# Decode attention mixed with a feed-forward branch: three small weight loads cut into sixteen pieces each

## The chip, the cores and the metric

The kernel runs on one core of one Trainium2 chip. The metric is the device time of one execution in microseconds (us); of several executions the median is shown.

## What is computed

One token, two branches, and a gate between them (the reference, cut to what matters):

```python
x = A_x                                              # 1 x 1 x 512
g = sigmoid((x * gate_w).sum(-1))
q = (x @ wq).reshape(1, 1, 32, 128)                  # 32 heads of 128
s = einsum("bhqd,bhkd->bhqk", q, k_cache) * 128 ** -0.5   # 65536 keys a head
p = softmax(s)
o = einsum("bhqk,bhkd->bhqd", p, v_cache)
a = o.reshape(1, 1, 4096) @ wo                       # wo: 4096 x 512
b = (silu(x @ w_gate) * (x @ w_up)) @ w_down
out = g * a + (1 - g) * b
```

All data are bf16. The caches are 32 heads x 65536 positions x 128 numbers each for keys and for values: 512 MiB each, a gigabyte together, and every byte of them is used once. Everything else is small beside that; `wo` has 4 MB.

## The kernel before, in words

**Tiles.** A head's keys are cut into four tiles, so there are 128 key tiles and 128 value tiles. Each is 128 partitions x 16384 numbers, 4 MB, and is fetched by one transfer (`load`, line 103, the issue is line 109). Every partition's share is one stretch of 32 KB in memory. All big tiles come from one pool of five buffers (`ring`, line 58), so a load has to wait until an earlier tile has been used up.

**Work on a key tile** (step n): VectorE multiplies it by the query (`products`, line 218) and folds 128 columns to 16 by three additions (line 222). TensorE adds up the rest with an identity matrix into the scores (`scores`, line 232). When a head's four tiles are through, its softmax follows (lines 243 to 272) on VectorE, ScalarE and TensorE.

**Work on a value tile** (step v): TensorE multiplies it by the probabilities, 32 matmuls (`values`, line 280). After a head's four value tiles, `head_out` (line 289) gathers the head's output into `oT`, and `project` (line 309, matmul line 310) multiplies it by the rows of `wo` that belong to the head and adds that to the sum `a_ps`.

**The order is written out by hand** (lines 319 to 370). A step issues the load of key tile n, then (in some steps) a load of `wo`, then the load of value tile v, and then the work. All loads are issued by SyncE, in this order, on one queue. SyncE does nothing else: an issue that has to wait holds up everything that is issued after it.

**The load of wo.** `wo` is fetched in eight groups of four heads (`load_wo`, line 143; the issue is line 146). A group is a tile of 128 partitions x 4 x 512 numbers, 512 KB: partition p gets, for each of four heads, one row of 1 KB. There are two such buffers (line 61). Group 0 is loaded at the start (line 148). The others are loaded in the loop (lines 334 and 335), when v is 8 more than a multiple of 16, thus eight value tiles before the first head that needs the group. In the queue this transfer stands between a key tile and a value tile.

**Semaphores.** Nothing in the kernel's text says which semaphore a transfer uses; the layer that builds the program deals them out. In the built program the transfers that SyncE issues take turns on eight semaphores, called DMAHW0 to DMAHW7. Where a semaphore's previous transfer isn't known to have landed, the next transfer on it is issued only when it has.

Of the kernel before, what the change touches and what calls it, by code (L numbers as in the profile page):

```python
# [11 lines left out]
P = 128  # L12
# [7 lines left out]

LAG = 8
SPREAD = 40


@with_exitstack
def kernel(
# [14 lines left out]
    nc = tc.nc  # L41
# [3 lines left out]
    _, H, Sk, Dh = A_k_cache.shape  # L45
# [94 lines left out]
    WG = 4  # L140
    wo_tiles = {}

    def load_wo(g):
        wo_tiles[g] = wo_pool.tile([P, WG, D], bf16, name="wo_sb")
        rows = A_wo[g * WG * P : (g + 1) * WG * P, :]
        nc.sync.dma_start(out=wo_tiles[g], in_=rows.rearrange("(h p) n -> p h n", p=P))

    load_wo(0)

    def feed_forward_in():  # L150
# [170 lines left out]
    for n in range(N):  # L321
        due = n >= G and not (n >= SPREAD and n % 4 == 3 and n - v < LAG)
        steps.append((n, v if due else None))
# [6 lines left out]
    for n, v in steps:  # L330
        if n is not None and n > 1:
            load(K_tiles, A_k_cache, n, "K_t")
        if v is not None:
            if v % (WG * G) == 2 * G and v // (WG * G) + 1 < H // WG:
                load_wo(v // (WG * G) + 1)
            load(V_tiles, A_v_cache, v, "V_t", (0, NB) if v < N - 1 else (0, 64, 96, 112, NB))
# [70 lines left out]
```

## Time and profile before

| what | value |
|---|---|
| median of 3 runs | 2549.31 us (2547.87 to 2550.05) |
| profiled execution, its own time | 2551.07 us |
| its span, first to last instruction | 2549.3 us |
| moved by the DMA engines | 1088.61 MB, mean 427 GB/s |
| VectorE busy | 2175.0 us, 85% |
| TensorE matmul busy | 1736.2 us, 68% |
| ScalarE busy | 75.7 us, 3% |
| key and value loads | 4096 KB each, median 35.4 and 29.6 us from issue to landing |
| loads of wo | 8 of 512 KB, median 36.3 us from issue to landing |
| share of the chain that ended last | DMA 66%, TensorE 22%, VectorE 11% |

The span is what lies between the first and the last instruction; the execution's own time is 1.8 us longer. "Landing" is the moment at which the last part of a transfer has been reported by its semaphore. The time from issue to landing is mostly time in the queue behind earlier transfers. Engines are named as in the profile: PE is TensorE, DVE is VectorE, ACT is ScalarE, SP or SPq is SyncE and its queue. An L with a number is a line of the kernel.

### The profile page before, as it was taken

What the parts mean: (1) busy time and instruction counts of PE and PEld (TensorE: products, weight loads), DVE (VectorE), ACT (ScalarE), POOL (GpSimd) and SP (SyncE); (2) the same over time, 40 slices, a digit from 0 to 9 for tenths busy, and PEclk for the clock granted to TensorE, in tenths of its full rate; (3) what the DMA queues carried; (4) which work ended last, traced back from release to release, by engine and by line L of the source; (5) the groups of instructions that cost most, each with busy time, mean ns of one, the idle gap of its engine ahead of it and who ended that gap; (6) DMA issues with size and microseconds to landing.
All of it is one profiled execution on the core that took longest, in us unless ns stands there. A gap on an engine that the chain in (4) does not pass through costs nothing.

```text
span 2549.3 us, 15203 instructions
## 1 busy us (share of the span) xinstructions
PE 1736.2 (68%) x6722; PEld 707.5 (28%) x6722; DVE 2175.0 (85%) x780; ACT 75.7 (3%) x206; POOL 0.7 (0%) x6
## 2 busy tenths in 40 slices
PE   3576666776776666666676776677667676776678
PEld 2232222222232222222222222222222222232223
DVE  6999888888888999998888888888888888888860
ACT  1000000000000000000000000000000000000000
POOL 0000000000000000000000000000000000000000
PEclk7677767777777677777776777767777777777779
DMA  9999999999999999999999999999999999999997
GB/s 407 427 432 430 430 433 429 433 428 431 432 431 431 428 431 431 432 430 432 430 430 433 429 432 429 433 429 432 431 429 433 429 433 428 433 430 432 430 434 304
DMA packets 42451, 1088.61 MB, mean 427 GB/s; under 512 B 4625, under 2 KB 8722, under 8 KB 8978
## 3 DMA queue, kind: packets, MB, share of 16 engines
q1 hardware_dynamic: 42386, 1087.66, 99.4%
q8 instruction: 52, 0.85, 0.1%
q14 instruction: 13, 0.11, 0.0%
HBM read 1087.64 MB, written 0.00 MB: 427 GB/s over the span
## 4 chain that ended last, share of the span: by engine, by line
DMA 66%; PE 22%; DVE 11%; issue 1%; ACT 0%; SPq 0%; DVEq 0%; ACTq 0%
DMA V_t<-in_A_v_cache_dram 60%; PE O_ps L280 20%; DVE K_t L218 6%; DMA K_t<-in_A_k_cache_dram 5%; DVE K_t L222 5%; PE S_ps L232 1%; DMA wq_t<-in_A_wq_dram 0%; PE qg_ps L118 0%; PE oh_ps L298 0%; DVE m L244 0%; ACT P_sb L257 0%; PE a_ps L205 0%; ACT O_sb L293 0%; DVE top L253 0%; PE a_ps L310 0%
## 5 line engine op out<-in xcount | busy, mean ns | idle before, releaser
L280 PE MATMUL O_ps<-V_t,P_sb 128*4 128x512 bf16 x4096 | 1156.4, 452 | 501.6 <-DMA V_t<-in_A_v_cache_dram 499.3
L218 DVE TENSOR_TENSOR K_t<-K_t,q_bc 128x16384 bf16<-128x16384 bf16 (+1 forms) x159 | 1117.2, 7026 | 275.3 <-DMA K_t<-in_A_k_cache_dram 272.1
L222 DVE TENSOR_TENSOR K_t<-K_t 128x2048 bf16<-128x2048 bf16 (+3 forms) x477 | 1030.6, 2161 | 14.2
L280 PEld LDWEIGHTS <-P_sb 128*4 128x4 bf16 x4096 | 394.0, 97 | 1244.4 <-issue 900.2
L232 PE MATMUL S_ps<-K_t,ident_b 128*128 128x128 bf16 x2048 | 464.5, 392 | 119.0 <-DVE K_t L222 119.0
L232 PEld LDWEIGHTS <-ident_b 128*128 128x128 bf16 x2048 | 225.7, 114 | 342.1 <-issue 149.2
L298 PE MATMUL oh_ps<-ident_f,O_sb 4*128 4x1 f32 x256 | 57.1, 340 | 73.1 <-ACT O_sb L293 73.1
L248 PE MATMUL mT_ps<-diag,ones_f 128*128 128x128 f32 x64 | 25.0, 494 | 78.3 <-ACT diag L246 78.3
L298 PEld LDWEIGHTS oh_ps<-ident_f,O_sb 4*128 4x128 f32 x256 | 54.4, 310 | 83.2 <-ACT O_sb L293 78.9
L246 ACT ACTIVATE diag<-ident_f,m 128x128 f32<-128x128 f32 x32 | 12.9, 402 | 2108.8 <-DVE m L244 2108.8
L295 DVE COPY O_sb<-O_ps 4x256 f32<-4x256 f32 x1 | 0.4, 413 | 56.5 <-ACT O_sb L293 56.5
L248 PEld LDWEIGHTS mT_ps<-diag,ones_f 128*128 128x128 f32 x64 | 15.7, 305 | 94.0 <-ACT diag L246 94.0
L244 DVE TENSOR_REDUCE m<-S_ps 128x1 f32<-128x512 f32 x32 | 21.9, 684 | 7.6 <-PE S_ps L232 7.6
L293 ACT ACTIVATE O_sb<-O_ps 4x512 f32<-4x512 f32 (+1 forms) x32 | 18.1, 565 | 135.4 <-PE O_ps L280 135.4
L257 ACT ACTIVATE P_sb<-S_ps,bias 128x512 bf16<-128x512 f32 x32 | 22.0, 687 | 1.0
L118 PE MATMUL qg_ps<-wq_t,X_bc 128*128 128x512 bf16 x32 | 8.8, 443 | 14.0 <-DMA wq_t<-in_A_wq_dram 14.0
L183 PE MATMUL b_ps<-wd_t,hT 128*1 128x512 bf16 x14 | 6.1, 626 | 15.7 <-DVE hT L176 15.7
L271 DVE RECIPROCAL recip<-tot_ps 128x1 f32<-128x1 f32 x32 | 5.1, 160 | 12.4 <-PE tot_ps L266 12.4
L310 PE MATMUL a_ps<-wo_sb,oT 128*1 128x512 bf16 x32 | 13.3, 416 | 0.4 <-ACT oT L305 0.4
L266 PEld LDWEIGHTS tot_ps<-rowsum,ones_f 128*128 128x128 f32 x64 | 9.5, 188 | 14.0 <-issue 14.0
L266 PE MATMUL tot_ps<-rowsum,ones_f 128*128 128x1 f32 x64 | 12.2, 260 | 0.0
L305 ACT ACTIVATE oT<-oh_ps,rg 128x1 bf16<-128x1 f32 x32 | 8.4, 264 | 75.3 <-PE oh_ps L298 75.3
(38 smaller groups left out, 62.4 us busy)
## 6 DMA issues: line engine op xcount, KB each, us to landing
K_t<-in_A_k_cache_dram SPq DMA_DIRECT2D x128, 4096.0 KB, 35.4
V_t<-in_A_v_cache_dram SPq DMA_DIRECT2D x127, 4096.0 KB, 29.6
wq_t<-in_A_wq_dram SPq DMA_DIRECT2D x1, 4096.0 KB, 12.3
wo_sb<-in_A_wo_dram SPq DMA_DIRECT2D x8, 512.0 KB, 36.3
V_t<-in_A_v_cache_dram SPq DMA_DIRECT2D x1, 2048.0 KB, 31.4
gu_t<-in_B_w_gate_dram SPq DMA_DIRECT2D x1, 1792.0 KB, 34.6
gu_t<-in_B_w_up_dram SPq DMA_DIRECT2D x1, 1792.0 KB, 38.4
wd_t<-in_B_w_down_dram SPq DMA_DIRECT2D x1, 1792.0 KB, 42.2
```

What stands on the lines that cost most here:

```text
L218: yield nc.vector.tensor_tensor(out=K, in0=K, in1=q_rep, op=ALU.mult)
L222: yield nc.vector.tensor_tensor(out=K[:, :, 0:half], in0=K[:, :, 0:half], in1=K[:, :, half : 2 * half], op=ALU.add,)
L232: nc.tensor.matmul(S_tiles[h][:, g * NB : (g + 1) * NB], lhsT=ident_b, rhs=K_tiles[n][:, :, c], start=(c == 0), stop=(c == WIDTH - 1),)
L244: nc.vector.tensor_reduce(out=m, in_=S_tiles[h], axis=AXIS.X, op=ALU.max)
L246: nc.scalar.activation(out=diag, in_=ident_f, func=ACT.Copy, scale=m)
L248: nc.tensor.matmul(mT_ps, lhsT=ones_f, rhs=diag, start=True, stop=True)
L257: nc.scalar.activation(out=P_tiles[h], in_=S_tiles[h], func=ACT.Exp, bias=bias, scale=scale, accum_out=rowsum[:, h : h + 1],)
L266: nc.tensor.matmul(tot_ps, lhsT=ones_f, rhs=rowsum[:, h : h + 1], start=True, stop=True)
L280: nc.tensor.matmul(O_tiles[h], lhsT=P_tiles[h][:, g * NB + j : g * NB + j + 4], rhs=V_tiles[n][:, j : j + 4, :], start=(g == 0 and j == 0) ...
L293: nc.scalar.activation(out=O_sb[:, :cut], in_=O_ps[:, :cut], func=ACT.Copy)
L298: nc.tensor.matmul(oh_ps, lhsT=O_sb[:, c * Dh : (c + 1) * Dh], rhs=ident_f[0:4, c : c + 1], start=(c == 0), stop=(c == 3),)
L310: nc.tensor.matmul(a_ps, lhsT=oT[:, h : h + 1], rhs=wo_tiles[h // WG][:, h % WG, :], start=False, stop=(h == H - 1),)
```

## The change

Groups 5, 6 and 7 of `wo` are no longer fetched by one transfer of 128 partitions each, but by sixteen transfers of eight partitions each (32 KB). Groups 0 to 4 are as they were. Destination, data and place in the order are the same.

```diff
+NARROW = 3
...
     def load_wo(g):
         wo_tiles[g] = wo_pool.tile([P, WG, D], bf16, name="wo_sb")
         rows = A_wo[g * WG * P : (g + 1) * WG * P, :]
-        nc.sync.dma_start(out=wo_tiles[g], in_=rows.rearrange("(h p) n -> p h n", p=P))
+        rows = rows.rearrange("(h p) n -> p h n", p=P)
+        step = P if g < H // WG - NARROW else 8
+        for a in range(0, P, step):
+            nc.sync.dma_start(out=wo_tiles[g][a : a + step], in_=rows[a : a + step])
```

`H // WG` is 8. In the changed kernel the issue of a load of `wo` is line 151, and that of a key or value load is line 111.

## The prediction

> **What bounds the kernel now.** I read the page's slices and queues first, to see which resource never rests; then SyncE's timeline around a load of wo, with the landing of each transfer, since the change lies there; then the chain of waits over the same stretch; last the built order of both kernels, which says what each issue waits for.
>
> The page, sections 2 and 3:
>
> ```profile
> DMA  9999999999999999999999999999999999999997
> q1 hardware_dynamic: 42386, 1087.66, 99.4%
> ```
>
> The 16 DMA engines are busy in every slice, and SyncE's queue alone fills 99.4% of them. VectorE, the next, has 85%. A microsecond in which the DMA engines have nothing to do is a microsecond on the end, unless the queue can later run faster than it does now.
>
> SyncE's timeline around group 5 of wo (start, duration, what):
>
> ```profile
> 1489.65 0.33 SPq L109 DMA_DIRECT2D V_t<-in_A_v_cache_dram  x1
> 1493.21 0.33 SPq L109 DMA_DIRECT2D K_t<-in_A_k_cache_dram  x1
> 1493.59 0.43 SPq L146 DMA_DIRECT2D wo_sb<-in_A_wo_dram  x1
> 1507.92 0.33 SPq L109 DMA_DIRECT2D V_t<-in_A_v_cache_dram  x1
> 1511.48 0.33 SPq L109 DMA_DIRECT2D K_t<-in_A_k_cache_dram  x1
> 1527.87 0.33 SPq L109 DMA_DIRECT2D V_t<-in_A_v_cache_dram  x1
> ```
>
> The landings of the first five, asked for one by one, took 29.1, 35.3, 36.4, 31.8 and 37.9 us from issue. So they landed at 1518.75, 1528.5, 1530.0, 1539.7 and 1549.4 us: a 4 MB tile every 9.7 us, and 1.5 us for wo. The queue is never empty: when the key tile lands at 1528.5, wo, a value tile, a key tile and another value tile (issued 1527.87) are already behind it. Groups 6 and 7 show the same picture at 1807.56 and 2121.51 us.
>
> The chain of waits over this stretch:
>
> ```profile
> 1489.65 29.10 DMA V_t<-in_A_v_cache_dram
> 1518.75 0.04 issue
> 1518.79 9.06 PE O_ps L280 x32
> 1527.85 0.02 issue
> 1527.87 31.25 DMA V_t<-in_A_v_cache_dram
> ```
>
> A value tile lands, TensorE uses it in 9.06 us, and that frees the buffer for the next value load but one. This loop looks like a TensorE step in the chain, but its long part is time in a full queue.
>
> **The change, part by part.** The order of PE, DVE, ACT and POOL is the same in both built programs; only SyncE's differs: three issues go, 48 come.
>
> *The issues alone.* 16 issues at wo's 0.43 us plus about 0.05 between issues (1493.21 to 1493.59 is 0.38 for an issue of 0.33) are 7.7 us. SyncE is free from 1494.0 to 1507.9, 13.9 us, in the old kernel. Without waits this costs nothing; uncovered, SyncE would be late by 7.7 us with over 20 us of work queued, still nothing.
>
> *The waits.* The built order of the changed kernel shows what matters (the semaphore that an issue waits for, in brackets; each of the three groups is alike):
>
> ```
> L111 K_t   [DVE, PE]
> L151 wo 0  -            wo 1 [DMAHW5]   wo 2  -           wo 3 [DMAHW7]
> L151 wo 4  [DMAHW0]     wo 5 [DMAHW1]   wo 6  [DMAHW2]    wo 7 [DMAHW3]
> L151 wo 8  [DMAHW4]     wo 9 [DMAHW5]   wo 10 [DMAHW6]    wo 11 [DMAHW7]
> L151 wo 12 [DMAHW0]     wo 13 [DMAHW1]  wo 14 [DMAHW2]    wo 15 [DMAHW3]
> L111 V_t   [DMAHW4, PE]
> L111 K_t   [DMAHW5, DVE, PE]
> ```
>
> Eight semaphores are dealt out in turn, and each issue waits for the landing of the transfer eight before it. Tile loads in the old kernel never feel that: fewer than eight are in flight. Sixteen pieces go around twice. Piece 7 is the eighth after the key tile issued just before the group, and waits for that tile to land. Queued behind it on SyncE are eight pieces and then the value and key loads that used to go out at 1507.92 and 1511.48.
>
> Call T0 the landing of that key tile (1528.5 for group 5). Pieces 0 to 6 are issued before T0 and stand in the queue behind the tile. At T0 the queue holds nothing but them.
>
> 1. Piece 7 goes out at T0 + 0.05. Pieces 8 to 14 wait for 0 to 6, which land right behind the tile; 0 to 6 are 7/16 of a transfer that took 1.5 us on 16 engines, so they are through within about 1.5 us even on half the engines, while pieces 8 to 14 leave one by one. Piece 15 waits for piece 7, which by the row of xT (1 KB, 1.8 us from issue to landing) lands near T0 + 2; its turn comes at T0 + 3.9. So nothing waits twice, and nine issues (7 to 15) of 0.48 us take 4.3 us.
> 2. The value load goes out at T0 + 4.4. Its buffer is long free (its old issue, 1507.92, is T0 - 20.6); DMAHW4 is piece 8, landed by T0 + 3.
> 3. Into an idle queue, a 4 MB transfer takes 12.3 us from issue to landing (wq at the start, behind two 1 KB loads). It lands at T0 + 16.7.
> 4. In the old kernel it lands at 1539.7, T0 + 11.2, behind wo's 1.5 us.
> 5. The loss is 5.5 us a group. The pieces' own transfer time lies inside that gap.
>
> After the gap the key load and the next value and key loads follow (their buffers were free at 1511.48, 1527.87 and 1531.42, all before T0 + 5), so four tiles stand in the queue by T0 + 6, and the value load after them waits, as before, for the first one's landing plus 9 us of TensorE. From there all is the old pattern, 5.5 us later. VectorE, with 85%, isn't what could regain it; nor the queue: 32 tiles of 9.7 and a wo of 1.5 are 311.9 us, and groups lie 313.95 us apart. The queue has at most 2 us in 314 to give back, under 6 us for all three groups.
>
> Sum: 3 x 5.5 = 16.5 us. The profiled execution took 2551.07 us, so its like would take 2567.6; it lies 1.76 us above the median, and the forecast on the median's scale is 2549.31 + 16.5 = **2565.8 us**, +0.65%. (About 0.2%, 5.1 us, is what a measurement of this kernel can tell from no change.)
>
> *Bounds of the unknown sizes.* An issue of eight partitions is not in the trace. Below: 0.33 us plus 0.05, as a tile's; above: 0.48 (the early issues) plus 0.05 and 0.02 for a wait (the row of wait instructions on L109 has a median of 17 ns); far above: 1.52, the slowest issue of the run (a key load at 22.84). I take wo's own 0.43, the same three-step pattern. The start into an idle queue: 9.7 plus xT's 1.8 is 11.5 below, wq's 12.3 above. With both low, 3.4 + 0.05 + 11.5 - 11.2 = 3.8 us a group, 11 in all; with both high, 6.1 and 18. The 2 us of slack can take up to 6 off the low end: 2549.3 + 5 to 2549.3 + 18, and more if an issue is dearer.
>
> *How many DMA engines.* The old transfer's 1.5 us are 512 KB on 16 engines. If eight partitions reach only eight, a group takes 3.0 us on these and nothing on the others. In the gap of some 6 us that is hidden; without a gap it would cost between -1.5 us a group (pieces on engines that run ahead) and +1.5. I take 0.
>
> [...]
>
> **The rivals.**
>
> *No wait that counts (not slower).* Piece 7's wait would have to end early: the semaphore would be one whose last transfer had landed by about 1505. The place is that issue; its price is the whole 16.5 us; the deciding point is whether the next value load goes out before T0 - 2 or so, when the queue runs dry. For it: 13.9 us of free SyncE time, and 7.7 us of issues fit. Against it: the built order names DMAHW3, the tile's. It gives 2549.3, between 2545 and 2554 by the engine count.
>
> *Every piece pays a landing.* If pieces 7 to 15 go one after another, 9 x 1.8 = 16.2 us before the value load, 16.2 + 12.3 - 11.2 = 17.3 a group, 52 in all: 2601. For it: each does wait for a landing. Against it: for the one eight before it.
>
> *A dear issue.* At 1.52 + 0.05 us, nine take 14.1: 15.2 a group, 46 in all: 2595. For it: that one row. Against it: 1 KB and one-row issues at 0.39 and 0.32.
>
> **How the numbers follow.** The gap at T0 with a loss of 3 to 8 us a group: 0.83, and 2565.8 us. No wait that counts: 0.07 (0.06 within 0.2%, 0.01 faster). Every piece pays a landing, 0.05; a dear issue, 0.05. The first alone gives the range: 2556 (low sizes and the slack regained) to 2575 (8.5 us a group, an issue of some 0.8 us); 0.80 or a little over lies inside. Slower by over 0.2%: the first but for a corner of 0.02, and the last two: 0.91. Within 0.2%: 0.08. Faster: 0.01.
>
> **What would show it.** SyncE's timeline: seven issues of L151 soon after the key load or as older tiles land, a long pause, then nine in a row from the key tile's landing, 0.4 to 0.5 us apart, and the value load right behind them. The DMA share must dip in three windows, by 5 to 6 us each. The value load should land 12 us after its issue in place of 32. It would be wrong if the nine stand 1.5 us or more apart, if the value load goes out some 14 us after the key load as it does now, or if the queue regains the gap before the end.

## The result, and the profile after

| | before | changed |
|---|---|---|
| median of 6 runs, us | 2548.80 | 2562.80 |
| lowest to highest, us | 2547.87 to 2550.05 | 2561.56 to 2564.55 |
| ratio, 95% interval | | 1.0052 (1.0041 to 1.0062) |
| span of the profiled execution, us | 2549.3 | 2560.7 |

The changed kernel is slower by 14.0 us, 0.52%. The forecast was +16.5 us (2565.8, range 2556 to 2575).

The mean rate of each fortieth of the span, first in the kernel before, then in the changed kernel, and the changed kernel's queue (the page's sections 2 and 3):

```profile
GB/s 407 427 432 430 430 433 429 433 428 431 432 431 431 428 431 431 432 430 432 430 430 433 429 432 429 433 429 432 431 429 433 429 433 428 433 430 432 430 434 304
GB/s 409 427 430 429 432 430 431 432 429 431 431 431 432 428 432 432 430 433 429 431 431 431 431 376 433 429 430 433 389 433 432 431 430 395 431 430 433 432 429 355
q1 hardware_dynamic: 42722, 1087.66, 99.1%
```

The bytes are the same. Apart from the last slice, in which the loads end, three slices drop, to 376, 389 and 395 GB/s: these are the three groups, and between them the rate is what it was. SyncE's queue fills 99.1% in place of 99.4%.

SyncE's timeline around group 5 of the changed kernel (L151 is the load of wo, L111 a tile load; the sixteen pieces are one row, from the first issue to the end of the last):

```profile
1492.83 0.33 SPq L111 DMA_DIRECT2D K_t<-in_A_k_cache_dram  x1
1493.20 38.27 SPq L151 DMA_DIRECT2D wo_sb<-in_A_wo_dram  x16
1531.58 0.36 SPq L111 DMA_DIRECT2D V_t<-in_A_v_cache_dram  x1
1532.04 0.36 SPq L111 DMA_DIRECT2D K_t<-in_A_k_cache_dram  x1
1532.50 0.38 SPq L111 DMA_DIRECT2D V_t<-in_A_v_cache_dram  x1
1532.98 0.47 SPq L111 DMA_DIRECT2D K_t<-in_A_k_cache_dram  x1
```

The value load that went out at 1507.92 goes out at 1531.58, and then four tile loads leave within 1.9 us, because their buffers had been free for a while. What SyncE does in those 38 us is in the chain of waits of the same stretch (start, duration, what):

```profile
1492.83 35.61 DMA K_t<-in_A_k_cache_dram
1528.43 0.02 issue
1528.45 0.27 SPq L151
1528.72 0.04 issue
1528.77 0.30 SPq L151
...
1531.17 0.30 SPq L151
```

The key tile issued at 1492.83 lands at 1528.43 (T0). 0.02 us later SyncE issues piece 7, and then eight more, 0.34 us apart. Only then comes the value load. In the list of SyncE's waits, two rows are new (waiting line, what ended the wait, us in total, times, longest):

```profile
SPq L151 <- DMA K_t<-in_A_k_cache_dram: 57.9, 6, 10.0
SPq L151 <- DMA V_t<-in_A_v_cache_dram: 42.6, 6, 9.4
```

Pieces 4 to 7 of each group wait for tiles to land: twelve waits. The stretch in windows (start and end; busy us and instructions of PE, PEld, DVE, ACT and POOL; granted clock; DMA share; GB/s), first the changed kernel:

```profile
1520.00:1527.00 7.00, 7.00 (x28) 2.52 (x27) 5.32 (x3) 0.00 (x0) 0.00 (x0) 0.82 0.64 240
1527.00:1534.00 7.00, 4.00 (x19) 1.71 (x16) 5.47 (x3) 0.40 (x1) 0.00 (x0) 0.91 0.45 125
```

and the kernel before:

```profile
1520.00:1527.00 7.00, 7.00 (x27) 2.52 (x26) 5.79 (x3) 0.00 (x0) 0.00 (x0) 0.80 0.97 403
1527.00:1534.00 7.00, 4.39 (x20) 1.88 (x18) 5.42 (x3) 0.35 (x1) 0.00 (x0) 0.93 1.01 425
```

The DMA share falls to 0.64 and 0.45 where it was 0.97 and 1.01. It falls before T0 already: the 16 engines don't keep step (the first of the key tile's sixteen marks comes 7.6 us before the last here; see the last section), and those that are ahead run dry first. What counts is the last one, at T0.

The landings are in the trace's records of the semaphores: a tile leaves sixteen marks on its semaphore, and the last of them is its landing (us; T0 is the landing of the key tile before the group):

| group | key tile after the tile before it | value load issued | value tile lands | before: key tile / value tile |
|---|---|---|---|---|
| 5 | +10.17 | T0 + 3.14 | T0 + 15.37 | +9.74 / T0 + 11.19 |
| 6 | +10.14 | T0 + 3.14 | T0 + 15.41 | +9.75 / T0 + 11.17 |
| 7 | +10.24 | T0 + 3.14 | T0 + 15.30 | +9.74 / T0 + 11.18 |

So each group loses 4.2 us after T0 and 0.4 us before it, 13.8 us in three. At the end of the loads the changed kernel is 13.8 us behind, counted from the tile before group 5. The two profiled spans differ by less, 11.4 us: that tile had landed 0.5 us earlier in the changed kernel's trace, and the last 64 value matmuls took 15.66 us in the profiled execution of before, at a granted clock of 0.89, and 13.97 in the other, at 1.00. The medians differ by 14.0.

### The profile page after: what moved, and what is told of

Same layout as the page of the kernel before. It is cut to its first block, busy times and chain, and to the rows that moved or that the text cites. A ratio compares the mean times of both kernels' runs of the same rounds, so it can differ in the third digit from the quotient of the medians.

```text
span 2560.7 us, 15251 instructions
## 1 busy us (share of the span) xinstructions
PE 1734.4 (68%) x6722; PEld 707.1 (28%) x6722; DVE 2175.0 (85%) x780; ACT 75.7 (3%) x206; POOL 0.7 (0%) x6
## 3 DMA queue, kind: packets, MB, share of 16 engines
q1 hardware_dynamic: 42722, 1087.66, 99.1%
## 4 chain that ended last, share of the span: by engine, by line
DMA 67%; PE 21%; DVE 11%; issue 1%; SPq 0%; ACT 0%; DVEq 0%; ACTq 0%
DMA V_t<-in_A_v_cache_dram 58%; PE O_ps L285 19%; DMA K_t<-in_A_k_cache_dram 8%; DVE K_t L223 5%; DVE K_t L227 5%; PE S_ps L237 1%; DMA wq_t<-in_A_wq_dram 0%; PE qg_ps L120 0%; PE oh_ps L303 0%; SPq L151 0%; DVE m L249 0%; ACT P_sb L262 0%; SPq L111 0%; PE a_ps L210 0%; ACT O_sb L298 0%
## 5 line engine op out<-in xcount | busy, mean ns | idle before, releaser
L188 PE MATMUL b_ps<-wd_t,hT 128*1 128x512 bf16 x14 | 6.0, 621 | 15.4 <-DVE hT L181 15.4
L271 PE MATMUL tot_ps<-rowsum,ones_f 128*128 128x1 f32 x64 | 12.2, 260 | 0.0
```

The source lines that it names most:

```text
L271: nc.tensor.matmul(tot_ps, lhsT=ones_f, rhs=rowsum[:, h : h + 1], start=True, stop=True)
```

## The experiments

Theory: the eighth transfer after the key load waits for that tile's landing; the queue drains; then nine issues and the start of a transfer into an idle queue pass before data flow again. Rivals: small pieces or many issues cost in themselves; running on eight of 16 DMA engines is the cost.

All runs change groups 5 to 7 alone unless told otherwise. The last column is how far the last tile's landing lags behind that of before, counted from the tile before group 5; in pool and all7 pieces move before that tile, so none is given.

| run | pieces of a group | median against before, us | ratio, 95% interval | loads' lag, us |
|---|---|---|---|---|
| changed kernel | 16 x 8 partitions | +14.0 | 1.0041 to 1.0062 | 13.8 |
| p6 | 6 of 16 or 32 partitions | +11.8 | 1.0034 to 1.0059 | 10.7 |
| p8 | 8 x 16 partitions | +7.9 | 1.0021 to 1.0043 | 7.7 |
| p32 | 32 x 4 partitions | +29.2 | 1.0100 to 1.0128 | 29.8 |
| cols16 | 16 x 128 partitions | +16.0 | 1.0049 to 1.0074 | 15.8 |
| spread | 16 x 8, two a step | +22.0 | 1.0067 to 1.0095 | 23.6 |
| pool | 16 x 8, by GpSimd | +16.0 | 1.0051 to 1.0076 | |
| all7 | 16 x 8, seven groups | +34.5 | 1.0122 to 1.0150 | |
| spread_stride | 16 x 8, every fourth partition, two a step | +11.2 | 1.0031 to 1.0056 | 11.4 |
| spread_dst | the same, rows read as in spread | +11.2 | 1.0028 to 1.0056 | 11.5 |
| six128 | 6 x 128 partitions | +0.6 | 0.9995 to 1.0012 | 0.3 |
| eight128 | 8 x 128 partitions | +5.1 | 1.0009 to 1.0027 | 4.4 |
| stride16 | 16 x 8, every fourth partition | +23.0 | 1.0077 to 1.0105 | 22.7 |

### First: the number of pieces

```diff
-        step = P if g < H // WG - NARROW else 8
-        for a in range(0, P, step):
-            nc.sync.dma_start(out=wo_tiles[g][a : a + step], in_=rows[a : a + step])
+        cuts = [0, P] if g < H // WG - NARROW else [0, 16, 32, 48, 64, 96, P]   # p6; p8: steps of 16, p32: of 4
+        for a, b in zip(cuts[:-1], cuts[1:]):
+            nc.sync.dma_start(out=wo_tiles[g][a:b], in_=rows[a:b])
```

p6: 

> Groups 5 to 7 of wo in six pieces (four of 16 partitions, two of 32). Theory (the eighth transfer after the last key load waits for that key tile, and the queue runs dry): the value load is the seventh after the key load and waits for nothing late, only the next key load is the eighth; it may go out at the tile's landing with a whole value tile still queued. No dip, median within 3 us of the kernel before (ratio 0.999 to 1.001). Rival (cutting costs in itself, by issues or by small descriptors): 6/16 of the 14 us, about +5 us. [...]

p8: 

> Groups 5 to 7 of wo in eight pieces of 16 partitions. Theory: the eighth piece waits for the key tile (T0), the value load goes out one issue later at T0 + 0.4 us and lands 12.2 us after that, 12.6 against 11.2 before: a gap of 1.4 us a group, +4.2 us in all, in the trace a value load issued 0.4 us after the key tile's landing. Rival (cost by number of pieces): half of 14, +7 us, with the value load issued long before the landing. [...]

p32: 

> Groups 5 to 7 of wo in 32 pieces of four partitions. Theory: after T0 come 25 issues of 0.34 us, 8.5 us, then the value load: 8.5 + 12.2 - 11.2 = 9.5 us a group, +28.6 us in all; the waits of pieces 16 to 31 cost nothing, since eight issues (2.7 us) take longer than a piece's landing (1.9 us). Rival (every piece pays its landing): 25 x 1.9 = 47 us a group, +145. Rival (the drain alone counts, pieces are free): as sixteen, +13.

p32 came out as the theory has it: 25 issues after T0, 0.35 us apart, value load at T0 + 8.7, +29.2 us. Pieces don't pay their landing (1.9 us from issue) one after another. p8 has the value load at T0 + 0.43 as expected, but it costs 7.9 and not 4.2 us: the key tile came 10.7 us after the tile before it, a microsecond late. And p6 contradicts the theory as it stood. Its value load goes out 12.2 us before the key tile lands, the queue never drains, and it is 11.8 us slower all the same. The key tile lands 12.3 to 12.6 us after the tile before it. Something other than a wait is at work there. SyncE's timeline in p6 (T0 is 1530.14):

```profile
1492.29 0.33 SPq L111 DMA_DIRECT2D K_t<-in_A_k_cache_dram  x1
1492.66 15.78 SPq L151 DMA_DIRECT2D wo_sb<-in_A_wo_dram  x6
1517.90 0.35 SPq L111 DMA_DIRECT2D V_t<-in_A_v_cache_dram  x1
1530.21 0.35 SPq L111 DMA_DIRECT2D K_t<-in_A_k_cache_dram  x1
```

```diff
+        cuts = [0, D] if g < H // WG - NARROW else list(range(0, D + 1, D // 4))   # cols16
+        for h in range(WG if len(cuts) > 2 else 1):
+            for a, b in zip(cuts[:-1], cuts[1:]):
+                heads = slice(h, h + 1) if len(cuts) > 2 else slice(0, WG)
+                nc.sync.dma_start(out=wo_tiles[g][:, heads, a:b], in_=rows[:, heads, a:b])
```

cols16: 

> Groups 5 to 7 of wo in sixteen pieces of all 128 partitions (128 columns of one head each, 256 B a row), so every piece reaches all 16 DMA engines. Theory: same order and same waits as sixteen pieces of eight partitions, so the same gap: value load issued some 3 us after the key tile's landing, 4.2 us a group, +12.5 us by landings and 11 to 15 us in the median; a little more if an issue of 128 rows is dearer than 0.34 us. Rival (eight of 16 engines are the cost): most of it gone, under +4 us.

Here every piece is 128 columns of one head and leaves sixteen marks of landing, as a tile does and where the changed kernel's pieces leave eight, so I take it to reach all 16 engines; and the cost is as large, 16.0 us against 14.0. The rival of the eight engines falls as the cause of the gap. The key tile is on time (9.8 us), the value load goes out at T0 + 4.24, since an issue of 128 rows takes 0.47 us and not 0.34.

### Second: the same pieces without the wait

```diff
-        step = P if g < H // WG - NARROW else 8
-        for a in range(0, P, step):
-            nc.sync.dma_start(out=wo_tiles[g][a : a + step], in_=rows[a : a + step])
+        if g < H // WG - NARROW:
+            nc.sync.dma_start(out=wo_tiles[g], in_=rows)
+            return
+        for a in range(0, P, 8):                                    # spread
+            pieces.append((wo_tiles[g][a : a + 8], rows[a : a + 8]))
...
+            for _ in range(2 if pieces else 0):                     # in each step, after load_wo
+                piece, rows = pieces.pop(0)
+                nc.sync.dma_start(out=piece, in_=rows)
```

spread: 

> The same 48 pieces of eight partitions, but two a step over eight steps, in place of sixteen in one step. Issues, sizes, descriptors and the engines used are those of the changed kernel; only what lies eight transfers back is now some 39 us old and has landed. Theory: no wait that counts, no dip, within 4.5 us of the kernel before, the rest being what 64 KB in place of 32 on half of the engines does to the slowest one (-1.5 to +1.5 us a group). Rival (issues or small pieces cost): +11 to 15 us as the changed kernel.

In pool, the queue of the narrow pieces is GpSimd's (`nc.gpsimd` for `nc.sync`).

pool: 

> The sixteen pieces of groups 5 to 7 are issued by GpSimd, which has nothing else to do. They take turns on eight semaphores of that queue and wait for each other as before, but no key or value load stands behind them. Theory: SyncE's order is free of wo, no dip, within 4.5 us of the kernel before. Rival (the pieces themselves cost, wherever they are issued): +11 to 15 us.

Both expectations failed. In spread no wait that counts holds up a tile load (the value load goes out 20 to 21 us before T0, as in the kernel before), and yet it is 8 us slower than the changed kernel: each of 48 pieces costs about half a microsecond. pool, where no tile load stands behind a piece, is 16.0 us slower than the kernel before. "Take the wait away and the cost is gone" is false. The trace's DMA packets, the single stretches that a DMA engine moves, show where the time goes. A stretch of 32 KB, one partition's share of a tile, takes 1.22 us where only tiles are under way (the median in the kernel before). Of those that overlap a packet of a narrow piece, 1372 of 2494 take over 1.3 us in spread, and 321 of 377 in p6, up to 2.3 us there. In p6 the pieces' own packets of 1 KB slow down too, from a median of 46 ns to 74. The windows show it without the packets. First the kernel before and spread, in the stretch of group 5's pieces:

```profile
1490.00:1650.00 160.00, 108.80 (x422) 44.57 (x421) 137.40 (x49) 4.23 (x12) 0.00 (x0) 0.77 1.01 432
1490.00:1650.00 160.00, 109.36 (x396) 42.93 (x395) 133.75 (x48) 4.23 (x12) 0.00 (x0) 0.71 1.00 416
```

Then p6 and six128 (below), which differ only in how a group is cut:

```profile
1520.00:1532.00 12.00, 10.46 (x44) 4.10 (x42) 6.64 (x4) 0.00 (x0) 0.00 (x0) 0.92 1.05 303
```
```profile
1520.00:1532.00 12.00, 9.91 (x43) 3.92 (x41) 9.01 (x5) 0.00 (x0) 0.00 (x0) 0.93 1.06 431
```

In all four the DMA engines are busy all the time. In p6 they move 303 GB/s, in six128 431. A full DMA share is no proof of full speed.

all7 (`NARROW = 7`): 

> Groups 1 to 7 in sixteen pieces each, in place of 5 to 7. Theory: 4.2 us for each group alike, since nothing is regained between them: 7 x 4.2 = +29 us, seven dips, each with a value load 3.1 us after the key tile's landing. Rival (part of each gap is regained in the stretch until the next, so that only the last ones show): under +20 us.

34.5 us for seven groups, 4.9 each: nothing is regained between groups. It is more than 4.2 each, as the key tile before a group is late in each of them (10.0 to 10.6 us).

### Third: which partitions, and which side

The new theory: pieces that are written into few neighbouring partitions crowd each other and the tile that streams beside them.

```diff
-        for a in range(0, P, 8):
-            pieces.append((wo_tiles[g][a : a + 8], rows[a : a + 8]))
+        for a in [b + c for b in range(0, P, 32) for c in range(4)]:          # spread_stride
+            pieces.append((wo_tiles[g][a : a + 29 : 4], rows[a : a + 29 : 4]))
```

spread_stride: 

> As spread (two pieces of eight partitions a step, +22 us), but a piece takes every fourth of 32 partitions in place of eight neighbours. Number of pieces, bytes, issues, waits and number of DMA engines stay. Theory now (eight or sixteen engines writing into a few neighbouring partitions are in each other's way and in that of the tile streaming beside them): most of the 22 us goes, -4.5 to +6 us remain. Rival (a small piece beside a streaming tile costs about 0.5 us by itself, wherever it lands): +22 us as spread.

spread_dst (piece n reads `rows[8 * n : 8 * n + 8]`): 

> As spread_stride on the destination side, every fourth of 32 partitions, but each piece is read from eight neighbouring rows of wo (four times) as in spread. The rows of wo in a group are therefore permuted among the partitions, so the last three groups are multiplied with the wrong rows. If the cost is on the side that is written: as spread_stride, -4.5 to +6 us. Rival (the cost is on the side that is read, eight neighbouring rows of memory at once): +22 us as spread.

stride16 (the same pieces, all in one step): 

> The changed kernel with every piece taking every fourth of 32 partitions in place of eight neighbours. The waits are those of the changed kernel. Theory: the gap stays (value load T0 + 3.1, landing T0 + 15.3: 4.15 us a group), and the 0.45 us by which the key tile before it was late goes: +12.5 us by landings, 11 to 14 in the median. Rival (the crowding makes the gap): under +5 us.

With every fourth partition half of spread's cost goes: 11.2 in place of 22.0 us. The window of spread_stride:

```profile
1490.00:1650.00 160.00, 110.42 (x416) 44.29 (x415) 136.56 (x49) 4.23 (x12) 0.00 (x0) 0.74 1.00 425
```

The 32 KB stretches beside a piece have a median of 1.22 us again, where spread's have 1.31. But 604 of 2291 still take over 1.3 us (398 of 2125 in spread_dst): the crowding is less, and not gone. Reading neighbouring rows or scattered ones makes no difference to the time, 11.2 us in both runs. So the half that went was crowding on the side that is written. The size was missed: at most +6 was expected. Of the 3.8 us a group that are left, about 1.9 fit the engines' load, by an estimate that has these pieces run on eight engines too: 16 pieces at 0.21 us (the last marks of pieces 0 to 6 of the changed kernel's group 5 are that far apart) are 3.4 us, where a group in one transfer took 1.5 before. What makes the other 1.9 was not separated; stretches that are still slow are one candidate. It comes while the pieces move: the lag of a group grows no further after its last piece, apart from a step of 1.5 us that the kernel before takes too, about once in 40 tiles (see the last section), and not at the same tile.

stride16 missed in size, and bears out the theory in kind. The key tile is on time (9.7 us), so what made it late was the crowding of neighbours. But an issue with such a step takes over twice as long (duration ns min/median/max); the nine last pieces of group 5 in stride16, and in the changed kernel:

```profile
L153 SPq DMA_DIRECT2D wo_sb<-in_A_wo_dram x9: 665/669/670, 1529.1 to 1534.8; - x9
```
```profile
L151 SPq DMA_DIRECT2D wo_sb<-in_A_wo_dram x9: 272/299/302, 1528.5 to 1531.2; - x9
```

Nine issues 0.72 us apart put the value load at T0 + 6.5, its landing at T0 + 18.8, 7.6 us a group and 22.7 in all; the median rose by 23.0.

six128 and eight128 take the crowding out and ask for the wait alone:

```diff
...
+        for h, a, b in [(0, 0, D), (1, 0, D)] + [(h, a, a + D // 2) for h in (2, 3) for a in (0, D // 2)]:
+            nc.sync.dma_start(out=wo_tiles[g][:, h, a:b], in_=rows[:, h, a:b])   # eight128: h in 0 to 3
```

six128: 

> Groups 5 to 7 in six pieces as in p6 (+11.8 us), same order and same waits, but each piece covers all 128 partitions (two of a whole head, four of half a head). Theory: no wait that counts and no crowding on few partitions: key tile 9.7 us after the value tile before it (12.4 in p6), at most 0.2 us for each added piece, 0 to +3 us in all. Rival (six pieces cost by their number or by the late key load): +11.8 as p6.

eight128: 

> As six128 (six pieces over all 128 partitions, no change in time), but eight pieces, each half a head. Theory: with two pieces more, the last one is the eighth transfer after the key load and waits for that tile's landing T0; the value load goes out at T0 + 0.5 us, and not 9.7 us before T0 as in six128. It lands at T0 + 12.8 against 11.2 before: 1.6 us a group, 4.7 us in all by landings. Rival (the number of pieces sets the cost, no step between six and eight): within 1 us of six128.

SyncE's timeline, six128 and then eight128 (T0 is 1527.13 and 1527.82):

```profile
1491.63 0.33 SPq L111 DMA_DIRECT2D K_t<-in_A_k_cache_dram  x1
1492.00 15.82 SPq L153 DMA_DIRECT2D wo_sb<-in_A_wo_dram  x6
1517.46 0.33 SPq L111 DMA_DIRECT2D V_t<-in_A_v_cache_dram  x1
1527.21 0.33 SPq L111 DMA_DIRECT2D K_t<-in_A_k_cache_dram  x1
```
```profile
1491.81 0.33 SPq L111 DMA_DIRECT2D K_t<-in_A_k_cache_dram  x1
1492.19 35.98 SPq L153 DMA_DIRECT2D wo_sb<-in_A_wo_dram  x8
1528.27 0.37 SPq L111 DMA_DIRECT2D V_t<-in_A_v_cache_dram  x1
```

Two pieces more, and the value load goes out 0.45 us after T0 in place of 9.7 us before it. Six pieces cost nothing that can be measured, eight cost 5.1 us. The step lies where the count of eight semaphores puts it (seven pieces were not run).

With these, the time after T0 can be read as one law:

| run | issues after T0, spacing | value load issued | lands | less the 11.2 of before |
|---|---|---|---|---|
| eight128 | 1 x 0.43 | T0 + 0.44 | T0 + 12.9 | 1.7 |
| changed kernel | 9 x 0.35 | T0 + 3.14 | T0 + 15.4 | 4.2 |
| cols16 | 9 x 0.47 | T0 + 4.24 | T0 + 16.5 | 5.3 |
| stride16 | 9 x 0.72 | T0 + 6.5 | T0 + 18.8 | 7.6 |
| p32 | 25 x 0.35 | T0 + 8.7 | T0 + 21.0 | 9.8 |

The landing comes 12.2 to 12.6 us after the issue in every row. What differs is the issues.

## Why the prediction was right, and where it was off

**The wait** (steps 1 and 2) held in each detail: piece 7 leaves 0.02 us after the key tile's landing, the pieces after it don't wait a second time, the value load follows. six128 against eight128 shows that it is this wait and not the pieces' number.

**The size of an issue** was the mis-sized term. I took 0.48 us from the row of the old transfer; it is 0.35. Nine of them are 3.1 and not 4.3 us. This makes nearly the whole difference between 5.5 and 4.2 us a group. The nearest row had the same shape of pattern but 128 partitions; the low bound, 0.38, was the better guess.

**The start into an idle queue**, 12.3 us by the row of wq, measured 12.2 to 12.3.

**Nothing regained** held: all7 loses about as much in each of seven groups. The 2 us in 314 that the prediction let the queue give back were no slack: a tile takes 9.71 to 9.72 us and not 9.7, and the step of 1.5 us falls once between two of these groups in the kernel before. (The range's low end, 2556, also lies 1.7 us above the prediction's own low sum, 2549.3 + 5.)

**How many DMA engines, "I take 0"**, failed in kind. The pieces do seem to run on eight engines: a piece leaves eight marks of landing on its semaphore and one more 0.45 us after its issue starts, where a tile leaves sixteen. But in the changed kernel the cost isn't the number of engines. It is the crowding on few partitions, which the step did not have: +0.4 us a group, as the seven early pieces meet the end of the key tile. stride16 has as many partitions in a piece and the same seven pieces ahead of T0, and its key tile isn't late (9.7 us). The two errors, -1.3 and +0.4 a group, partly cancel: 16.5 - 3.9 + 1.2 is 13.8, the lag of the loads. That the sum isn't further off is in part luck.

**The rival "no wait that counts"** was mispriced. I put it at 2549.3, between 2545 and 2554. Measured without the wait, the same pieces cost 22.0 us more than before (spread). The likely reason that the changed kernel pays less, argued and not tested by itself: nine of its sixteen pieces move in the gap, while the tiles stand still, and have nobody to crowd.

A version faster than both kernels wasn't found. six128 equals the kernel before.

## What to carry to other kernels

Count the transfers that a queue can have under way before an issue must wait for a landing (eight here), and put a cut-up load only where the eighth transfer back has long landed; the price of getting it wrong is the drained queue, that is every issue after the landing plus the start of the next transfer (here 12.2 to 12.6 us for a tile that follows its predecessor by 9.7 in a full queue). A transfer cut by partitions was not free here even without a wait (22.0 us for 48 pieces in spread): cut small loads along the columns, so that each piece spans all partitions (six such pieces cost nothing here; more of them without a wait were not run). And a DMA share of 1.0 says that the engines are occupied; the GB/s beside it say whether they are fast (a share of 1.05 at 303 GB/s in p6, 1.06 at 431 in six128).

## What the runs showed of the hardware that I had not expected

- The DMA engines don't keep step. In the kernel before, the first of a tile's sixteen marks comes 7.6 us before the last at group 5 and 12.2 us at the end; the lead grows in steps of about 1.5 us, one in some 40 tiles. The cause of the steps is open. A drained queue resets it: 0.4 us after group 5 of the changed kernel, 1.9 at its end. It isn't a gain, since the last engine sets the landing.
- SyncE's time for an issue differed with the shape of the pattern: 0.30 us for 8 partitions x 4 x 512 (changed kernel), 0.33 for a tile, 0.43 for 128 x 4 x 512 (both in the kernel before) or 128 x 128 (cols16), 0.67 for eight partitions with a step of four (stride16).
- A 32 KB piece of eight partitions into an idle queue (piece 8 of group 5 in the changed kernel) took 1.9 us from issue to landing, about as long as the 1.8 us of xT's 1 KB.
